# Scores and sums folded into the runs of values from block 4 on, with the output's halves in another order, in a fused attention and bilinear feed-forward kernel

## The chip, the cores and the metric

One core of one Trainium2 chip. The metric is the time of one execution on the device in microseconds (us), lower is better. Executions of one kernel scatter over 1 to 2 us within a session. The span of a profile is 1.8 us shorter than the time of the same execution (302.3 against 304.1 for the kernel before), because the time also holds what lies outside the first and last instruction.

## The reference

```
q, k, v: (8, 8, 576, 64) fp32; w_a, w_b: (512, 1536); w_out: (1536, 512)
attention within chunks of 64 positions:
    attn = softmax(q k^T / 8);  o = attn v          # 64x64 per chunk and head
x = o as 4608 tokens x 512
y = ((x w_a) * (x w_b)) w_out                       # 4608 x 512, fp32
```

## The kernel before

The 4608 tokens go in 9 blocks of 512, the attention in 18 units of 256. TensorE (PE) does two kinds of work: matmuls on the full 128x128 array for the feed-forward, in a form with seven products in place of eight, and runs of small matmuls on four 64x64 tiles at once for the attention (values, scores and sums of a unit). Scores are q k^T, and their Exp on ScalarE (ACT) gives E. Sums are E times ones; two Ln and then the inverse (an Exp) on ACT make 1/sum of them. Values are E v, which VectorE (DVE) multiplies by that into x (xT). From block 2 on, a block is six groups, and a group issues its products in this order. `now` is the group itself; `last` is the group before, whose bank C is finished here.

```python
# cut: the loop over blocks K and groups i
now.p1()                       # bank A (pa); ACT then copies it to B (pb)
if last:
    last.add7()                # DVE: c_sb = pc + v_sb; then pc = pc + u_sb
chunk(chunks.get(K, chunks[4])[2 * i])          # c0 halves of the output of block K-1
if last:
    last.p3()                  # on pb; DVE multiplies pb by b_sb
attend(K, i, 0)                # attention work hung here; sums of x on DVE
now.p6()                       # on pb; ACT then copies it to u_sb
if last:
    last.p4()                  # on pc: needs add7's second instruction
    finish(last)
now.p2()                       # on pa; ACT then copies it to b_sb
chunk(chunks.get(K, chunks[4])[2 * i + 1])      # c1 halves
attend(K, i, 1)                # runs of values, scores, sums
now.p5()                       # on pb; ACT then copies it to v_sb
exps()                         # ACT: the second Exp of the scores
now.p7()                       # starts a new pc
last = now
```

The output of a block is seven products, n = 0 to 6, in two halves each: 14 halves, dealt out to the places c0 and c1 by the table `chunks`. After product 4 DVE does two instructions on its bank C (po):

```python
if n == (3 if one else 4):   # one: a form for the last block only
    nc.vector.scalar_tensor_tensor(out=rows(self.o1, hi), in0=halves(self.C),
        scalar=OUT_SCALE, in1=halves(self.v), op0=MULT, op1=ADD)      # o_sb<-po,vo_sb
    nc.vector.tensor_tensor(out=self.C, in0=self.C, in1=self.u, op=ADD)  # po<-po,uo_sb
```

`bring(U)` casts q, k and v of unit U to bf16 on POOL (GpSimd) and starts the loads of the next; `combine_x` makes four sums of x on DVE, each `s<-xT` or `s<-s,xT` (these "sums of x" are not the attention's sums). The kernel uses eight banks of PSUM, the memory that matmuls write: pa, two pb, pc, po, pq and two pt.

The softmax here doesn't subtract the row's maximum and nothing guards it: scores larger than these inputs give would overflow.

## Time and profile before

| | before |
|---|---|
| time, median of 3 | 303.82 us (303.5 to 304.27) |
| span of the profile | 302.3 us |
| PE, DVE, ACT, POOL busy | 97, 69, 65, 64% |
| runs on 64x64 tiles from block 4 on | 9.30 us, in 16 runs |
| PE waiting between full-tile matmuls, 90 to 284 us | next to nothing |

The prediction below reads the page. I show here only lines that it doesn't show: PE in group 4 of the kernel before (start in us, duration, engine, line, operation, output<-inputs, tile, number of matmuls):

```profile
191.97 1.47 PE L578 MATMUL pq<-wo,so 128*128 128x256 f16 x12
193.28 0.60 PE L440 MATMUL pb<-s,wa 128*128 128x256 f16 x4
193.72 0.60 PE L440 MATMUL pb<-s,t 128*128 128x256 f16 x4
194.16 0.60 PE L440 MATMUL pc<-xT,t 128*128 128x256 f16 x4
```

The way to read these: the lines are two output halves, p3, p6 and p4. Durations overlap (p3 is 0.60 long, and p6 starts 0.44 after it), so the difference of two starts is the cost; where it is longer than the matmuls between need, I call the excess a step. 193.72 - 193.28 = 0.44 is one product of four matmuls, and 193.28 - 191.97 = 1.31 two output halves. No line carries a bracket with a wait.

### The profile page before, as it was taken

To read this page: it belongs to the slowest core of one execution; us is meant where nothing else is said; L and a number is where in the kernel's file an instruction comes from. 1 tells how busy PE (TensorE), PEld (TensorE's weight loads), DVE (VectorE), ACT (ScalarE), POOL (GpSimd) and SP (SyncE) were. 2 spreads that over 40 slices of the span, in tenths; PEclk is the share of its full clock that TensorE was granted. 3 is DMA by queue.
4 is the path that set the end of the run, shared out by engine and by line. 5 is a ranking of instruction groups with operands and counts; after the bars stand their busy time and mean duration, and the time that the engine had idled before them with its cause. 6 is when DMAs were issued, how large, how long until landed. Compare 5 with 4: busy or idle time off the path is not lost.

```text
span 302.3 us, 8608 instructions
## 1 busy us (share of the span) xinstructions
PE 292.4 (97%) x3527; PEld 231.9 (77%) x3527; DVE 210.0 (69%) x343; ACT 196.5 (65%) x355; POOL 193.3 (64%) x180
## 2 busy tenths in 40 slices
PE   6799999999999999999999999999999999999995
PEld 2344367866588888888888888888888888888884
DVE  3456575878767696769676966796679667965773
ACT  2643567348387768776867687768776876566532
POOL 0665758995999698808880888178817901780660
PEclk9999999999999999999999999999999999999999
DMA  7999999999999999896959395958721001100024
GB/s 222 307 382 284 283 336 345 242 217 210 219 239 262 213 242 276 188 210 181 208 122 245 129 205 132 210 163 198 123 87 72 2 2 69 73 0 3 2 98 179
DMA packets 141127, 54.29 MB, mean 180 GB/s; under 512 B 117152, under 2 KB 135200, under 8 KB 141088
## 3 DMA queue, kind: packets, MB, share of 16 engines
q1 hardware_dynamic: 140944, 53.69, 69.9%
q8 instruction: 27, 0.44, 0.6%
q14 instruction: 12, 0.10, 0.1%
q10 hardware_dynamic: 144, 0.07, 0.1%
HBM read 37.75 MB, written 9.44 MB: 156 GB/s over the span
## 4 chain that ended last, share of the span: by engine, by line
PE 83%; DMA 5%; SPq 4%; DVE 3%; POOL 1%; ACT 1%; issue 1%; DVEq 0%; ACTq 0%; POOLq 0%
PE pb L440 19%; PE pc L440 12%; PE pa L440 12%; PE po L578 12%; PE pq L578 10%; PE pb L651 3%; DMA st<-in_k_dram 3%; DMA st<-in_moe_w_b_dram 2%; PE po L390 2%; PE pc L390 2%; PE pa L390 2%; PE pq L390 2%; PE pt L328 2%; PE pt L295 2%; SPq L112 1%; SPq L194 1%
## 5 line engine op out<-in xcount | busy, mean ns | idle before, releaser
L520 POOL TENSOR_TENSOR so<-ab_sb 128x512 f16<-128x512 f16 x23 | 27.4, 1190 | 68.5 <-DVE ab_sb L490 68.5
L440 PEld LDWEIGHTS <-t 128*128 128x128 f16 x504 | 48.3, 98 | 8.4 <-issue 1.7
L440 PE MATMUL pb<-s,wa 128*128 128x256 f16 x336 | 50.5, 273 | 0.0
L440 PE MATMUL pa<-xT,wb 128*128 128x256 f16 x336 | 50.4, 273 | 0.0
L478 DVE TENSOR_TENSOR c_sb<-pc,v_sb 128x512 f32<-128x512 f32 x42 | 28.9, 687 | 27.7 <-ACT v_sb L451 27.7
L578 PEld LDWEIGHTS <-ab_sb 128*128 128x128 f16 x390 | 37.8, 98 | 5.2 <-issue 0.9
L440 PEld LDWEIGHTS <-wb 128*128 128x128 f16 x336 | 32.9, 98 | 4.0
L440 PEld LDWEIGHTS <-wa 128*128 128x128 f16 x336 | 31.8, 98 | 4.3 <-issue 0.2
L490 DVE SCALAR_TENSOR_TENSOR ab_sb<-pc,c_sb 128x512 f16<-128x512 f32 x42 | 29.0, 690 | 7.8 <-PE pc L440 6.3
L451 ACT COPY u_sb<-pb 128x512 f32<-128x512 f32 x42 | 24.7, 588 | 14.9 <-PE pb L440 14.7
L490 DVE SCALAR_TENSOR_TENSOR ab_sb<-pb,b_sb 128x512 f16<-128x512 f32 x42 | 28.9, 689 | 6.1 <-PE pb L440 5.2
L458 ACT COPY pb<-pa 128x512 f32<-128x512 f32 x42 | 24.1, 573 | 10.3 <-PE pa L440 10.0
L578 PEld LDWEIGHTS <-so 128*128 128x128 f16 x288 | 28.1, 98 | 3.4
L451 ACT COPY b_sb<-pa 128x512 f32<-128x512 f32 x42 | 25.0, 595 | 7.1 <-PE pa L440 7.1
L479 DVE TENSOR_TENSOR pc<-pc,u_sb 128x512 f32<-128x512 f32 x42 | 28.9, 688 | 0.0
L520 POOL TENSOR_TENSOR so<-so,ab_sb 128x512 f16<-128x512 f16 x23 | 27.4, 1192 | 1.7
L451 ACT COPY v_sb<-pb 128x512 f32<-128x512 f32 x42 | 24.7, 587 | 5.1 <-PE pb L440 4.4
L520 POOL TENSOR_TENSOR ab_sb<-ab_sb 128x512 f16<-128x512 f16 x23 | 26.8, 1166 | 0.0
L520 POOL TENSOR_TENSOR so<-ab_sb,so 128x512 f16<-128x512 f16 x23 | 26.1, 1163 | 0.0
L338 DVE TENSOR_TENSOR xT<-pt,ln 128x512 f16<-128x512 f32 x29 | 18.8, 685 | 9.9 <-PE pt L328 6.5
L440 PE MATMUL pb<-s,t 128*128 128x256 f16 x168 | 25.3, 273 | 0.0
L440 PE MATMUL pc<-xT,t 128*128 128x256 f16 x168 | 25.2, 272 | 0.1
(129 smaller groups left out, 574.4 us busy)
## 6 DMA issues: line engine op xcount, KB each, us to landing
out_dram<-o_sb SPq DMA_DIRECT2D x34, 256.0 KB, 2.3
st<-in_v_dram SPq DMA_DIRECT2D x32, 256.0 KB, 4.7
st<-in_k_dram SPq DMA_DIRECT2D x25, 256.0 KB, 4.5
st<-in_q_dram SPq DMA_DIRECT2D x23, 256.0 KB, 3.7
st<-in_moe_w_b_dram SPq DMA_DIRECT2D x6, 512.0 KB, 7.1
st<-in_moe_w_a_dram SPq DMA_DIRECT2D x6, 512.0 KB, 7.0
st<-in_moe_w_out_dram SPq DMA_DIRECT2D x6, 512.0 KB, 6.4
st<-in_q_dram SPq DMA_DIRECT2D x4, 512.0 KB, 5.7
```

The source lines that it names most:

```text
L295: nc.tensor.matmul(sm[cl][j * 64:j * 64 + 64, :], ones[cl * 64:cl * 64 + 64, :], E[cl * 64:cl * 64 + 64, j].rearrange("p m g s -> p (m g s)"),
L338: nc.vector.tensor_tensor(out=x.rearrange("p m (g c s) -> p m g c s", g=2, c=2)[:, m, :, cl, :], in0=av[cl][:, m], in1=rs[:, cl, m].rearra ...
L390: nc.tensor.matmul(ps[n], w_ab[n, i][:, kt, o:o + 128], xT[:, kt, c0:c1], start=(kt == 0), stop=(kt == NKT - 1),)
L440: nc.tensor.matmul(t[:, h * 256:h * 256 + 256], w[:, kt, h * 128:h * 128 + 128], x[:, kt], start=start and h == 0 and kt == 0, stop=h == 1 ...
L451: nc.scalar.copy(out=t, in_=src)
L458: nc.scalar.copy(out=self.B, in_=self.A)
L478: nc.vector.tensor_tensor(out=self.c, in0=self.C, in1=self.v, op=ADD)
L479: nc.vector.tensor_tensor(out=self.C, in0=self.C, in1=self.u, op=ADD)
L490: nc.vector.scalar_tensor_tensor(out=self.dst[:, :, c0:c0 + 256], in0=t.rearrange("p (h n) -> p h n", h=2), scalar=AB_SCALE, in1=o.rearran ...
L520: (eng or nc.gpsimd).tensor_tensor(out=o, in0=x0, in1=x1, op=op)
L578: nc.tensor.matmul(t[:, c0:c0 + 256][:, cols], a[:, kt, th * 128:th * 128 + 128], w[:, kt, cols], start=n in (0, 4) and first and kt == 0, ...
L651: nc.tensor.matmul(out_ps[K, tg], ab_tiles[K][:, ft, tg * 128:tg * 128 + 128], wo_sb[:, ft], start=(ft == 0), stop=(ft == NFT - 1),)
```

## The change

The intent is to have fewer runs on 64x64 tiles, as each pays a way in and a way out on PE (0.093 and about 0.11 us, worked out in the prediction). From block 4 on, the scores of the unit two on and the sums of the next unit go into the same run as the values. For that the scores move to bank pc and the sums to pa and one of po or pq, and the output's halves are placed so that those banks are free. The core of the diff:

```diff
+    late_ln = []
+
-    def sums(U, halves=None):
+    def sums(U, halves=None, pools=(None, None)):
         E = E_of[U]
-        sm = [bank() for _ in range(2)]
+        sm = [bank(p) for p in pools]
 # cut: with pools given, the second Ln goes to late_ln and is issued after the next p1
-                at(K, 0, 0, sums, U)
-            at(K, 1, 0, inverse, U)
+                if K == 3:
+                    at(K, 0, 0, sums, U)
+            if K == 4:
+                at(K, 0, 1, sums, U)
+                at(K, 0, 1, scores_beside(psum_c), U + 1)
+            at(K, 1, 1 if K == 4 else 0, inverse, U)
             at(K, 2, 1, values, U)
 # cut: K < 4 as before; from 4 on:
+                at(K, 2, 1, scores_beside(psum_c), U + 2)
+                at(K, 2, 1, sums_beside(psum_o), U + 1)
             at(K, 4, 1, values, U + 1)
+                at(K, 4, 1, scores_beside(psum_c), U + 3)
+                at(K, 4, 1, sums_beside(psum_q), U + 2)
 # the table of halves; a pair is (c1, c2), c2 being a new place between p5 and p7
-            4: (1, 1, 1, 1, 2, 1, 1, 2, 2, 0, 1, 1),
-            NBLK - 1: (1,) * 12,
+            3: (1, 1, 1, 1, 2, 1, 1, 2, 2, 0, 1, 1),
+            4: (0, 1, 1, (1, 1), 1, (1, 1), 1, 1, 1, (1, 1), 0, 1),
+            5: (1, 1, 1, (1, 1), 1, (1, 1), 1, 1, 1, (1, 1), 0, 1),
+            NBLK - 1: (1, 1, 1, (1, 1)) + (1,) * 8,
 # casts and loads on POOL and SP; cut: bring() takes the names to cast
-                    bring(2 * K + 4)
-                elif i == 3 and K > 2:
-                    bring(2 * K + 5)
+                    bring(2 * K + 4 if K < 4 else 2 * K + 5, "qkv" if K < 4 else "qk")
+                elif i == 3 and K == 3:
+                    bring(11)
                 elif i == 3:
 # cut: the lines that this one replaces
+                    bring(9, "qk") if K == 2 else cast(2 * K + 5, "v")
+                elif i == 5 and K > 2:
+                    bring(2 * K + 6)
 # product 5 of the output before product 4
-                        lambda g=g, n=n, th=th: g.part(n, th) for n in range(7) for th in range(2)
+                        lambda g=g, n=n, th=th: g.part(n, th)
+                        for n in (range(7) if K < 4 else (0, 1, 2, 3, 5, 4, 6))
+                        for th in range(2)
 # cut: the lines that read c0, c1 and c2 from the table; after p1, p2 and p5
-                chunk(chunks.get(K, chunks[4])[2 * i])
+                chunk(c0)
-                chunk(chunks.get(K, chunks[4])[2 * i + 1])
+                chunk(c1)
+                chunk(c2)
```

More of the change, by code (lines that the diff above doesn't have):

```diff
@@ L303, in sums @@
         rs_of[U] = ln_of[U]
+        ln = ln_of[U]
         for cl in range(2):
-            nc.scalar.activation(
-                out=ln_of[U][:, cl].rearrange("p m n -> p (m n)"), in_=sm[cl], func=AF.Ln
-            )
+            late_ln.append(
+                lambda cl=cl: nc.scalar.activation(
+                    out=ln[:, cl].rearrange("p m n -> p (m n)"), in_=sm[cl], func=AF.Ln
+                )
+            )
+        for cl in range(1 if pools[0] else 2):
+            late_ln.pop(0)()
             if halves:
@@ L355, in slot, with bring @@
             values(f)
-    def bring(U):
+    def bring(U, names="qkv"):
         if U >= NU:
@@ L363, in bring @@
         transpose_dma(U)
-        bring_v(U)
+        if "v" in names:
+            bring_v(U)
     def bring_v(U):
@@ L841, in scores_beside, with sums_beside @@
             return lambda u: scores(u, (pool, psum_b[0]), 1)
+        def sums_beside(pool):
+            return lambda u: sums(u, pools=(psum_a, pool))
         for K in range(2, NBLK):
@@ L851 @@
                 attention[K, 0, 1] = [lambda K=K: combine_x(K, (3,))]
-                at(K, 0, 0, sums, U)
-            at(K, 1, 0, inverse, U)
-            at(K, 2, 1, values, U)
-            at(K, 2, 1, scores_beside(psum_o), U + 1)
-            at(K, 3, 0, sums, U + 1)
+                if K == 3:
[4 more added lines that the diff above has]
+            at(K, 1, 1 if K == 4 else 0, inverse, U)
+            at(K, 2, 1, values, U)
+            if K < 4:
+                at(K, 2, 1, scores_beside(psum_o), U + 1)
+                at(K, 3, 0, sums, U + 1)
+            else:
+                at(K, 2, 1, scores_beside(psum_c), U + 2)
+                at(K, 2, 1, sums_beside(psum_o), U + 1)
             at(K, 3, 1, inverse, U + 1)
             at(K, 4, 1, values, U + 1)
-            at(K, 4, 1, scores_beside(psum_q), U + 2)
+            if K < 4:
+                at(K, 4, 1, scores_beside(psum_q), U + 2)
+            else:
+                at(K, 4, 1, scores_beside(psum_c), U + 3)
+                at(K, 4, 1, sums_beside(psum_q), U + 2)
             at(K, 5, 0, lambda u: combine_x(u // 2, (0,)), U + 1)
@@ L886 @@
                 if i == 1:
-                    bring(2 * K + 4)
-                elif i == 3 and K > 2:
-                    bring(2 * K + 5)
+                    bring(2 * K + 4 if K < 4 else 2 * K + 5, "qkv" if K < 4 else "qk")
+                elif i == 3 and K == 3:
+                    bring(11)
                 elif i == 3:
-                    cast(9, "qk")
-                    load(10)
-                    transpose_dma(9)
+                    bring(9, "qk") if K == 2 else cast(2 * K + 5, "v")
+                elif i == 5 and K > 2:
+                    bring(2 * K + 6)
                 if i == 0:
@@ L896 @@
                     outs += [
-                        lambda g=g, n=n, th=th: g.part(n, th) for n in range(7) for th in range(2)
-                    ]
+                        lambda g=g, n=n, th=th: g.part(n, th)
+                        for n in (range(7) if K < 4 else (0, 1, 2, 3, 5, 4, 6))
+                        for th in range(2)
+                    ]
+                steps = chunks.get(K, chunks[5])[2 * i:2 * i + 2]
+                c0, c1, c2 = steps[0], *(steps[1] if type(steps[1]) is tuple else (steps[1], 0))
                 now = Group(K, i)
                 now.p1()
+                while late_ln:
+                    late_ln.pop(0)()
                 if last:
                     last.add7()
-                chunk(chunks.get(K, chunks[4])[2 * i])
+                chunk(c0)
                 if K == 2 and i == 0:
```

## The prediction

> **What bounds the kernel now.** I read the page first: the busy line, the slices, the chain that ended last.
>
> ```profile
> PE 292.4 (97%) x3527; PEld 231.9 (77%) x3527; DVE 210.0 (69%) x343; ACT 196.5 (65%) x355; POOL 193.3 (64%) x180
> ...
> PE   6799999999999999999999999999999999999995
> ...
> PE 83%; DMA 5%; SPq 4%; DVE 3%; POOL 1%; ACT 1%; issue 1%; DVEq 0%; ACTq 0%; POOLq 0%
> ```
>
> PE is full from the second slice on and is 83% of the chain. The other engines stand at 64 to 69%, so they matter only where one of them makes PE wait. As matmul ends are modelled, "full" says little; I therefore read the timeline of PE by its start times (start, us, engine, line):
>
> ```profile
> 186.51 0.82 PE L578 MATMUL pq<-wo,so 128*128 128x256 f16 x6
> 187.16 0.60 PE L440 MATMUL pb<-s,wa 128*128 128x256 f16 x4
> 187.69 0.41 PE L295 MATMUL pt<-E,ones 64*64 64x512 bf16 x4
> 188.03 0.61 PE L440 MATMUL pb<-s,t 128*128 128x256 f16 x4
> ...
> 194.59 0.60 PE L440 MATMUL pa<-xT,wb 128*128 128x256 f16 x4
> 195.12 0.44 PE L328 MATMUL pt<-E,v_raw 64*64 64x64 bf16 x32
> 195.79 0.61 PE L440 MATMUL pb<-s,wa 128*128 128x256 f16 x4
> ```
>
> A half of an output product (x6) takes 187.16 - 186.51 = 0.65, a feed-forward product (x4) 0.437; both are 0.1093 a matmul. From 90 to 284 us I found no longer step between full-tile matmuls than that, beyond 0.04. The rest is the runs on 64x64 tiles. Sums alone: 188.03 - 187.16 - 0.437 = 0.436, of which entry is 0.093 and the rest two matmul pairs and the way out. Values with scores: 195.79 - 194.59 - 0.437 = 0.763. A block of six groups (from 184.52 to 214.47, both values) is 29.95, of which 27.6 is full-tile work, and the two kinds of runs 2 x (0.436 + 0.763) = 2.40.
>
> **What the Trainium skill says.** "TensorEngine Tiling (Array Packing)", Key Properties: "Changing tiling mode (not just tile) drains the TensorE". The trace agrees: each run pays 0.093 to get in, and after the last sums matmul 0.333 passes where its 512 columns alone take 0.22, so about 0.11 to get out. "TensorE: Matmul & The Clock Gate", Part 3, What overlaps and what doesn't: matmuls are strict FIFO; Architectural detail: ACT and DVE are strict FIFO too. So a matmul that waits holds up every later one, and a DVE instruction put ahead of another delays it. The trace shows both below. For what a matmul on these small tiles costs, I use the trace (32 in 0.253).
>
> **The change, part by part.** No instruction is added, dropped or resized on any engine. What moves is their order (I laid the two instruction lists side by side, engine by engine).
>
> 1. *Fewer runs.* From block 4 on there were 8 runs of sums, 7 of values with scores, 1 of values alone: 8 x 0.436 + 7 x 0.763 + 0.471 = 9.30. Now: sums 10 with scores 11; six runs of values, scores and sums; values 16 with sums 17; values 17. The turn from values to scores inside a run costs 0.763 - 0.471 - 0.253 = 0.04; I give the turn to sums 0.05. Appending sums then costs 0.05 + 0.010 + (0.333 - 0.119) = 0.274, where 0.119 is the old tail after scores: six runs x 1.037, two x about 0.74, and 0.471: 8.18. Gain **1.12 us**, 0.16 for each of seven runs saved. PE is the bound, so it counts in full.
>
> 2. *The fourth product of the output on DVE.* Its second half (po, the bank C) now runs between p5 and p7 of group 4, and group 5 has no half after its first product. When that bank is done, DVE has to do four things in order. The same four stand in the trace before, after two halves in group 3:
>
> ```profile
> 190.92 0.69 DVE L626 SCALAR_TENSOR_TENSOR o_sb<-po,vo_sb 128x512 f32<-128x512 f32 x1 [1.11 <-PE po L578]
> 191.65 0.70 DVE L630 TENSOR_TENSOR po<-po,uo_sb 128x512 f32<-128x512 f32 x1
> 192.25 0.68 DVE L478 TENSOR_TENSOR c_sb<-pc,v_sb 128x512 f32<-128x512 f32 x1
> 192.85 0.69 DVE L479 TENSOR_TENSOR pc<-pc,u_sb 128x512 f32<-128x512 f32 x1
> ```
>
> From the first start to the last end 2.62; it began 0.26 after the last matmul of po had given way (190.66 to 190.92). The product p4 accumulates into pc and so needs the last of the four. That it does wait can be seen where PE stalled early on:
>
> ```profile
> 86.46 0.69 DVE L479 TENSOR_TENSOR pc<-pc,u_sb 128x512 f32<-128x512 f32 x1
> ```
>
> ```profile
> 86.47 0.60 PE L440 MATMUL pb<-s,t 128*128 128x256 f16 x4
> 87.20 0.60 PE L440 MATMUL pc<-xT,t 128*128 128x256 f16 x4
> ```
>
> DVE ends at 87.15, PE goes on at 87.20: 0.05. In the old order PE had two more halves (1.31) in between, and p4 came at 194.16, after 193.54. In the new order only p7, p1, p3 and p6 lie between: 4 x 0.437 = 1.75. The chain is 0.26 + 2.62 + 0.05 = 2.93. PE idles 2.93 - 1.75 = 1.18 in group 5, in blocks 4, 5, 6 and 7: **4.7 us**. The missing half also leaves p6 waiting for ACT's copy of pa into pb (the copy starts 0.31 after the start of p1's last matmul, takes 0.57; p6 could have started 0.38 earlier), but that lies inside the same 1.18.
>
> 3. *The first group of block 4.* It has no half after p1 either, so p6 waits 0.38 for that copy. And its run is sums 10, then scores 11 into pc. ACT does two Ln first, then the Exp that frees pc for p7. In the trace ACT's Ln pair starts 0.43 after the sums (202.67 to 203.11) and each next instruction 0.49 later, so Exp ends at 0.43 + 0.98 + 0.60 = 2.01 from the sums' start; p7 is due at 0.27 + 0.25 + 0.12 + 0.437 = 1.08. Wait with the 0.05: 0.97. With 0.08 for p4 in the next group: **1.4 us**, once.
>
> 4. *The scores in pc elsewhere.* There Exp is the first on ACT and a half stands before p7. From the run's end Exp ends at 0.49, p7 is due at 1.09. Hidden. The Ln of pa ends at 0.99, p1 is due at 1.53. The second Exp and copy end near 2.77, p6 of group 3 is due at 3.06. Hidden, by 0.3.
>
> 5. *End.* In the last block C is now ready in group 5, so the pair of DVE instructions stands before the last pair of c_sb and pc: STT at 0.26, then as above, end 2.88 after p5's start, p4 due at 2.62: 0.31, against 0.04 before: **0.3 us**.
>
> 6. *Elsewhere.* In group 0 the last output eviction (0.69, 0.60 to the next) now stands between add7 and p3's multiply. I walk it: add7 at 0.43 and 1.04 after p1, eviction 1.64, multiply 2.24, one sum of x (0.41 to 0.65), multiply of pc to 3.9 to 4.2; p7 is due at 3.93. Up to 0.3 in five blocks; I take **0.4 us** in all. Casts moved on POOL: needed products lie 4 us or more after; loads and transposes keep some 14 us. Hidden.
>
> Sum: 303.8 - 1.1 + 4.7 + 1.4 + 0.3 + 0.4 = 309.5. As part 6 and a share of 3 may vanish in slack I did not see, I state 309.2, 1.8% slower.
>
> **The rivals.** *The intent wins*: the waits are hidden and only 1.1 is saved, 302.7. For it: the order of halves was plainly chosen to give banks time, and the same table shows care for p7. Against it: the four DVE instructions cannot be shortened, and nothing but four products covers them. *ACT becomes the bound around the merged runs*: the Ln moved ahead of v_sb and the copy. At 65% busy it has room, and the walk of part 4 leaves 0.3; if I mis-sized that by 0.3, 7 groups lose as much, 2 us more, 311. *Transfers*: scores a unit earlier need q and k earlier. The DMA is at 1.00 of its time around 110 us and 0.84 by 135, where the first of them is loaded; a late landing would hold up POOL, then the output, once, by a few us. POOL's idle stretch of 7.8 us a block speaks against it.
>
> **Range and chances.** The four stalls of part 2 are the surest term (each within 0.15, so 0.6); part 3 may be 0.8 to 1.8; part 6 zero to 1.5; the saving 0.8 to 1.5. Together 307.2 to 310.6 for 8 times in 10. The line of 2% lies at 309.9, just above my number: slower by over 2% three times in ten. Faster by 2% would need 6 us that a saving of at most 1.5 cannot give; I leave 0.02 for an error of mine in the whole reading.
>
> **What would show it.** In the profile after: runs of values, scores and sums of about 1.04; on PE in group 5 of blocks 4 to 7 a step of 1.2 us before p4 (pc<-xT,t), with the DVE instruction on pc,u_sb as its releaser; a wait of some 1 us for Exp on pc once, near 144 us; blocks of 29.95 - 0.32 + 1.2 = 30.8. No such step at p4 would prove part 2 wrong, and with it the number: blocks of 29.6 and 303. Steps at p6 or p1 released by ACT would favour the second rival, POOL or a DMA as releaser of the output's halves the third.

## The result, and the profile after

The changed kernel took 310.91 us (median of 4, 310.08 to 311.97) against 303.66 (303.34 to 304.27) for the kernel before in the same rounds: a ratio of 1.0238 (1.0202 to 1.0274). Ratios here are the recorded ones of the runs in the same rounds, with their 95% interval, so not quite the ratio of the medians I quote. Executions over 1.5% slower than the fastest of the same kernel are left out of the means. Two later sessions gave 1.0215 (1.0193 to 1.0237) and 1.0196 (1.0165 to 1.0226). So the change costs 6.0 to 7.2 us, and the first session's median lies 0.3 us above the range that I had given. Over the kernel before, that range was 3.4 to 6.8 us: 7.2 lies above it, the later 6.5 and 6.0 inside, so on which side the result fell was in part scatter.

PE's busy slices and the chain that ended last, on the page after:

```profile
PE   6699999999999999998999899989998999899995
...
PE 77%; DVE 7%; DMA 7%; SPq 4%; issue 1%; ACT 1%; POOL 1%; DVEq 0%; POOLq 0%
```

From the third slice to the last but one all were 9; now five are 8, each 7.7 us long: the one from 139 us on, at the turn from block 3 to 4, and those from 170, 201, 232 and 263 us on, one in each of blocks 4 to 7. And DVE's share of the chain has gone from 3 to 7%. The view of PE's waits says on what (who waited for whom: us in all, how often, the longest):

```profile
PE pc L448 <- DVE pc L487: 2.7, 5, 0.6
PE pb L448 <- ACT pb L466: 1.3, 5, 0.3
...
PE pc L448 <- ACT E L279: 0.8, 1, 0.8
```

In the kernel before, none of these stands among the twelve largest. The wait alone comes out less than the lost time (0.53 against 0.69 at p4 below), so I count by start times. Group 5 of block 5 on PE after (the output's half with product 4 ends here, as it ended before group 4 in the kernel before):

```profile
199.49 0.82 PE L586 MATMUL po<-wot,ab_sb 128*128 128x256 f16 x6
200.14 0.60 PE L448 MATMUL pc<-s,t 128*128 128x256 f16 x4
200.58 0.60 PE L448 MATMUL pa<-xT,wb 128*128 128x256 f16 x4
201.02 0.60 PE L448 MATMUL pb<-s,wa 128*128 128x256 f16 x4
201.89 0.60 PE L448 MATMUL pb<-s,t 128*128 128x256 f16 x4 [0.28 <-ACT pb L466]
203.02 0.60 PE L448 MATMUL pc<-xT,t 128*128 128x256 f16 x4 [0.53 <-DVE pc L487]
...
204.54 0.60 PE L448 MATMUL pb<-s,wa 128*128 128x256 f16 x4
205.29 0.60 PE L448 MATMUL pc<-s,t 128*128 128x256 f16 x4
```

p6 starts 0.87 after p3 instead of 0.44, p4 1.13 after p6: 0.43 and 0.69 lost, 1.13 together. The last two lines are p5 and p7: p7 starts 0.75 after p5, a step of 0.31. DVE in the same stretch of the same kernel:

```profile
200.34 0.69 DVE L634 SCALAR_TENSOR_TENSOR o_sb<-po,vo_sb 128x512 f32<-128x512 f32 x1 [0.44 <-PE po L586]
201.07 0.70 DVE L638 TENSOR_TENSOR po<-po,uo_sb 128x512 f32<-128x512 f32 x1
201.68 0.68 DVE L486 TENSOR_TENSOR c_sb<-pc,v_sb 128x512 f32<-128x512 f32 x1
202.27 0.69 DVE L487 TENSOR_TENSOR pc<-pc,u_sb 128x512 f32<-128x512 f32 x1
...
203.47 1.17 DVE L428 TENSOR_TENSOR s<-xT 128x512 f16<-128x512 f16 x1
204.56 0.68 DVE L498 SCALAR_TENSOR_TENSOR ab_sb<-pc,c_sb 128x512 f16<-128x512 f32 x1
```

This is the chain of four instructions that the prediction laid out, from 200.34 to 202.96, and PE goes on 0.06 later. What was not in it is the line before the last: a sum of x that takes 0.41 when alone took 1.17. The last line is the multiply that frees pc; it ended at 205.24, and p7 went on 0.05 later. POOL's instruction beside the sum, same kernel:

```profile
203.32 1.04 POOL L213 CAST v_raw<-st 128x1024 bf16<-128x1024 f32 x1
```

Blocks 6 and 7 have no casts in group 5, as the last of the 18 units has been cast before. There the same sum was short in both profiles of the changed kernel (0.41 to 0.42), and p7 had no step. Group 5 of block 6, profile after:

```profile
234.79 0.42 DVE L428 TENSOR_TENSOR s<-xT 128x512 f16<-128x512 f16 x1
```

From the run in group 2 of one block to that of the next it is 31.28 and 31.32 over the group 5 of blocks 4 and 5, and 30.82 over that of block 6; the prediction had 30.8 for all.

The merged run before that, on PE after (the scores' lines left out):

```profile
197.38 0.82 PE L586 MATMUL po<-wot,ab_sb 128*128 128x256 f16 x6
198.13 0.44 PE L335 MATMUL pt<-E,v_raw 64*64 64x64 bf16 x32
...
199.04 0.61 PE L448 MATMUL pb<-s,wa 128*128 128x256 f16 x4
```

It costs 199.04 - 197.38 - 0.655 (the half ahead of it) = 1.005, where values with scores (0.763) and sums alone (0.436) made 1.199 before: 0.19 saved here. The six merged runs took 1.00 to 1.05, so 0.15 to 0.19 each.

The whole account, from start times on PE (start minus start before minus the matmuls between). The second column of results is a second profile of the same changed kernel, whose time was 310.44:

| term | predicted | profile after | second profile |
|---|---|---|---|
| fewer runs (9.30 before; 8.05 and 8.00 after) | -1.12 | -1.25 | -1.30 |
| group 5 of blocks 4 to 7, p6 and p4 | +4.7 | +4.53 | +4.53 |
| turn from block 3 to 4: p7, p6, p4, p7 | +1.4 | +2.27 | +1.45 |
| end | +0.3 | 0.0 | 0.0 |
| p7 in group 5 of blocks 4 and 5, and in the group 0 after each | +0.4 | +1.04 | +1.05 |
| p4 in group 4 of blocks 4 to 7 | 0 | +0.43 | +0.42 |
| sum | 5.7 | 7.0 | 6.2 |
| measured from block 2's first values to the end, less 208.5 before | | 7.0 | 6.3 |

The last row leaves out the loading phase, which ends between 93.0 and 96.1 us in the profiles and so adds up to some 3 us that no kernel explains. At the end p4 waits 0.25 instead of 0.04 as predicted, but a later wait for po is 0.15 instead of 0.37, so nothing is left of it.

### The profile page after: what moved, and what is told of

The parts are those of the page before. It is cut to its first block, busy times and chain, and to the rows that moved or that the text cites. A ratio compares the mean times of both kernels' runs of the same rounds, so it can differ in the third digit from the quotient of the medians.

```text
span 309.0 us, 8602 instructions
## 1 busy us (share of the span) xinstructions
PE 293.6 (95%) x3525; PEld 232.0 (75%) x3527; DVE 212.2 (69%) x343; ACT 196.4 (64%) x355; POOL 193.5 (63%) x180
## 4 chain that ended last, share of the span: by engine, by line
PE 77%; DVE 7%; DMA 7%; SPq 4%; issue 1%; ACT 1%; POOL 1%; DVEq 0%; POOLq 0%
PE pb L448 16%; PE pc L448 12%; PE po L586 11%; PE pa L448 11%; PE pq L586 10%; DMA st<-in_q_dram 3%; PE pb L659 3%; DMA st<-in_v_dram 2%; PE po L398 2%; SPq L182 2%; DMA st<-in_moe_w_b_dram 2%; PE pa L398 2%; DVE c_sb L486 2%; PE pq L398 2%; DVE s L428 2%; DVE pc L487 2%
## 5 line engine op out<-in xcount | busy, mean ns | idle before, releaser
L528 POOL TENSOR_TENSOR so<-so,ab_sb 128x512 f16<-128x512 f16 x23 | 26.6, 1159 | 1.7
L448 PE MATMUL pc<-s,t 128*128 128x256 f16 x168 | 25.2, 272 | 1.3 <-ACT E L279 0.8
```

What stands on the lines that cost most here:

```text
L448: nc.tensor.matmul(t[:, h * 256:h * 256 + 256], w[:, kt, h * 128:h * 128 + 128], x[:, kt], start=start and h == 0 and kt == 0, stop=h == 1 ...
L528: (eng or nc.gpsimd).tensor_tensor(out=o, in0=x0, in1=x1, op=op)
```

## The experiments

Fourteen runs on three chips. My theory after the first look: the DVE chain in front of p4 costs 4.5 of the loss, the rest comes from POOL's casts that stretch DVE's sums of x, and from the turn into block 4. Rivals: the merged runs themselves (their banks and their work on ACT), and the loading of q and k a unit earlier.

**e1_casts: the casts moved away from group 5.**

```diff
                 if i == 1:
+                    if K >= 4:
+                        cast(2 * K + 4, "v")
                     bring(2 * K + 4 if K < 4 else 2 * K + 5, "qkv" if K < 4 else "qk")
-                elif i == 5 and K > 2:
-                    bring(2 * K + 6)
+                elif i == 4 and K > 2:
+                    bring(2 * K + 6, "qk")
```

> The changed kernel with the casts of q and k for the unit after next at the start of group 4, where POOL was idle, instead of group 5, and the cast of v two groups later. Nothing on PE, ACT or DVE moves. Theory (POOL's casts in group 5 stretch DVE's sums of x from 0.41 to about 1.2 us, so the multiply that frees pc comes late): the sums of x in groups 5 and 0 go back to 0.4 to 0.7, the steps of 0.3 before p7 in group 5 and most of 0.64 before p4 at the start of block 4 go; 1.2 to 1.9 us less than the changed kernel, near 309.3. Rival (DVE simply has too many instructions there): under 0.4 less, 310.5 or more. The step of 1.13 before p4 in group 5 stays under both.

Measured 311.32 us (311.01 to 312.82), before 304.27 (303.62 to 304.95): 1.0247 (1.0214 to 1.0281). In its trace the steps at p7 in group 5 of blocks 4 and 5 and after are gone, but the 0.64 before p4 at the turn stayed and the time did not fall: the expectation failed. As it had run beside the kernel before and not beside the changed one, I ran the same file twice more, below.

**e2_no_add: the second of the four DVE instructions taken out** (wrong: relative error 0.66).

```diff
-                nc.vector.tensor_tensor(out=self.C, in0=self.C, in1=self.u, op=ADD)
+                if one or not 3 <= self.K < 7:
+                    nc.vector.tensor_tensor(out=self.C, in0=self.C, in1=self.u, op=ADD)
```

> The changed kernel without the addition po<-po,uo_sb on DVE in blocks 4 to 7 (wrong result on purpose, 4 instructions of 0.60 from start to start fewer). Theory (the chain of four DVE instructions sets p4 in group 5): p4 in group 5 comes 0.60 earlier, so the steps before p6 and p4 together shrink from 1.13 to about 0.53, and the step before p7 may shrink by up to 0.3: 2.4 to 3.5 us less, near 308. Rival (ACT's copy of pa into pb, which makes p6 wait 0.44, or the long runs themselves hold PE): 1 us less or none, as only 0.69 of each 1.13 would be DVE's at most and the rest of the sum would reappear elsewhere.

Measured 308.74 us (308.22 to 308.92), 1.0143 (1.0124 to 1.0163), so 2.2 to 2.9 us less than the changed kernel at its 1.0215 to 1.0238 (2.4 to 3.5 were expected). PE in group 5, profile of e2_no_add:

```profile
201.97 0.60 PE L448 MATMUL pb<-s,t 128*128 128x256 f16 x4 [0.28 <-ACT pb L466]
202.41 0.60 PE L448 MATMUL pc<-xT,t 128*128 128x256 f16 x4
```

p4 follows p6 by 0.44, with no wait: the 0.69 is gone in all four blocks, 4 x 0.69 = 2.8. The wait of p6 for ACT stays at 0.44, as it should, since it has another cause. At p7 some shifted: the step in group 0 grew from 0.2 to 0.46, that in group 5 fell from 0.31 to 0.02. That the chain on DVE sets p4 is thereby shown, not only read.

**e3_split: the sums back in runs of their own**, everything else as changed.

```diff
-                if K == 3:
+                if K != 4:
                     at(K, 0, 0, sums, U)
-                at(K, 2, 1, sums_beside(psum_o), U + 1)
+                at(K, 3, 0, sums, U + 1)
-                at(K, 4, 1, sums_beside(psum_q), U + 2)
```

> The changed kernel with its order of halves, but sums 11 to 17 back in runs of their own in groups 3 and 0 (into the two pt banks); scores stay two units on. Theory (a saved run is worth what the trace says, 0.763 + 0.436 - 1.007 = 0.19): seven more runs cost 1.3, of which some 0.3 may come back since sums in group 0 give DVE time: 0.7 to 1.4 us more than the changed kernel, near 312. Rival (the merged runs bring new waits on ACT that eat their saving): no change or less, 311 or below.

Measured 311.12 us (309.92 to 312.21), 1.0224 (1.019 to 1.0257): level with the changed kernel, where 0.7 to 1.4 us more were expected. The runs cost 9.28 again, yet the steps at p7 were absent, and p4's at the turn into block 4 was 0.11 in this profile. The casts lay in group 5 as before, but in block 5 the sum of x began 0.10 ahead of the cast of v (202.00 against 202.10) and took 0.43. So the merging by itself is not what makes the kernel slower; its gain of 1.25 and the waits at p7 of about 1.0 nearly cancel. That is read from start times.

**e4_halves: the kernel before with only the table and the order of the halves changed.**

```diff
-            4: (1, 1, 1, 1, 2, 1, 1, 2, 2, 0, 1, 1),
-            NBLK - 1: (1,) * 12,
+            3: (1, 1, 1, 1, 2, 1, 1, 2, 2, 0, 1, 1),
+            4: (0, 1, 1, (1, 1), 1, (1, 1), 1, 1, 1, (1, 1), 0, 1),
+            5: (1, 1, 1, (1, 1), 1, (1, 1), 1, 1, 1, (1, 1), 0, 1),
+            NBLK - 1: (1, 1, 1, (1, 1)) + (1,) * 8,
 # and the order 0, 1, 2, 3, 5, 4, 6, and chunk(c2), as in the change
```

> The kernel before with only the new places and the new order of the output halves from block 4 on; scores one unit on, sums in their own runs, casts where they were. Theory (the order of halves is what costs: 1.13 in group 5 of four blocks, 0.4 at the start of block 4, 0.25 at the end, 0.1 to 0.3 elsewhere): 5 to 6.5 us more than the kernel before, near 309.3. Rival (halves alone are harmless, and the runs with their ACT and POOL order bring the loss): within 1.5 us of the kernel before.

Measured 309.57 us (309.33 to 310.12), 1.0176 (1.0156 to 1.0197): 5.35 us more than before. The steps on PE are the same 0.44 at p6 and 0.69 at p4 in each of four blocks, and 0.18 at p4 in group 4. At the turn into block 4 there is 0.05 only. The order of the halves alone makes three quarters of the loss or more.

**after_again: the changed kernel once more**, five rounds, as the basis for what follows on this chip.

> The changed kernel as it is, on the chip of the next three, since the profiled executions start their steady part up to 1.4 us apart and e1 needs a reference of the same chip. Expected 7.0 to 7.5 us over the kernel before if the first measurement was sound.

Measured 310.74 us (310.0 to 311.11), before 304.36 (303.15 to 304.95): 1.0215 (1.0193 to 1.0237), 6.5 us over it where 7.0 to 7.5 were expected. What its profile shows beside the first is told below.

**e5_old_halves: the changed kernel with the old order and nearly the old table.**

```diff
-            4: (0, 1, 1, (1, 1), 1, (1, 1), 1, 1, 1, (1, 1), 0, 1),
-            5: (1, 1, 1, (1, 1), 1, (1, 1), 1, 1, 1, (1, 1), 0, 1),
-            NBLK - 1: (1, 1, 1, (1, 1)) + (1,) * 8,
+            5: (1, 1, 1, 1, 1, (1, 1), 1, 2, 2, 0, 1, 1),
+            NBLK - 1: (1,) * 12,
-                        for n in (range(7) if K < 4 else (0, 1, 2, 3, 5, 4, 6))
+                        for n in range(7)
```

> The changed kernel with the order and the places of the output halves of the kernel before (one of three halves of group 2 stays between p5 and p7); merged runs, scores two units on and casts as in the changed kernel. Theory (the halves cost 5.4, of which the merged runs are innocent): no step before p4 in group 5; what stays is 1.3 of wait for Exp and some tenths at the start of block 4, up to 0.2 per merged run in group 4, where no half stands before p7, against 1.2 saved: 0 to 2 us over the kernel before, near 305. Rival (merged runs need the new order of halves, whose places were chosen for them): waits of 0.5 us and more at p7, p1 or p6 after each run, 4 us or more over the kernel before.

Measured 306.87 us (305.99 to 307.25), 1.0087 (1.0069 to 1.0106): 3.9 less than the changed kernel, but 2.6 over the kernel before where 0 to 2 were expected. No step before p4 in group 5. At the turn into block 4 the steps were 0.38, 0.36, 1.09, 0.30 and 0.40 (p7, p4, p7, p3, p4). And the merged run in group 4 now took 1.18 instead of 1.005, as the sums wait 0.17 for ACT's copy that frees pa; with that the merging in that group saves only 0.02 of 1.199. As I read it, this is what the new order of the halves bought: time for pa at one place, paid for on DVE at another.

**e6_old_casts: e5 with the casts of e1 and the scores of unit 11 put ahead of the sums of unit 10 in block 4.**

```diff
-                at(K, 0, 1, sums, U)
                 at(K, 0, 1, scores_beside(psum_c), U + 1)
+                at(K, 0, 1, lambda u: sums(u, pools=(psum_t, psum_t)), U)
 # and the edits of e1_casts and e5_old_halves
```

> As e5_old_halves, with the casts at the start of group 4 and, in the first group of block 4, scores 11 ahead of sums 10 and the second Ln after the next copy. Theory (saved runs are worth 1.2 once their waits are gone): the wait of 1 us for Exp falls to 0.1, steps before p7 go; 0.5 to 1.2 us less than the kernel before, near 303. Rival (a merged run moves its cost to ACT whatever the order): same as the kernel before or slower.

Measured 304.91 us (304.21 to 306.13 for the fast runs), 1.0026 (1.0002 to 1.005): not the 0.5 to 1.2 us less than the kernel before that was expected, but 0.8 more. One of its runs, the profiled one, took 310.57 and counts as slow. ACT and PE there, profile of e6_old_casts:

```profile
154.97 0.60 ACT L609 ACTIVATE o_sb<-po 128x512 f32<-128x512 f32 x1 [4.20 <-DMA out_dram<-o_sb]
```

```profile
157.03 0.95 PE L448 MATMUL pb<-s,wa 128*128 128x256 f16 x4 [4.27 <-ACT v_sb L459]
157.79 1.06 PE L448 MATMUL pb<-s,t 128*128 128x256 f16 x4
158.64 1.06 PE L448 MATMUL pc<-xT,t 128*128 128x256 f16 x4
```

A store of the output had been queued on SP behind a load and two transposes of the casts that I had moved; ACT needed its buffer, PE needed ACT. Then PE did four matmuls in 0.85 instead of 0.44, for about 3.4 us. The Trainium skill, "TensorE: Matmul & The Clock Gate", Part 1, What's actually happening, has PE's clock halved after one idle window of about 3.4 us and restored after a busy one of the same length; the trace agrees, with 4.3 us idle before it and a granted clock of 0.50 from 158 to 160 us. This is my edit's fault, not that of the change; whether the fast executions of e6 lost anything there is not shown.

**e7_casts_k4: the changed kernel with the casts of e1 and the turn of e6, the new halves kept.**

```diff
-                at(K, 0, 1, sums, U)
                 at(K, 0, 1, scores_beside(psum_c), U + 1)
+                at(K, 0, 1, lambda u: sums(u, pools=(psum_t, psum_t)), U)
 # and the edit of e1_casts
```

> The changed kernel with its own halves, casts at the start of group 4 and the first group of block 4 turned round as in e6. Theory: what is left over the kernel before is the halves' 5.4 less the 1.2 that runs save, plus 0.4 to 1 at the start of block 4: 4.5 to 5.2 us over the kernel before, 2 to 2.7 less than the changed kernel. Rival (time is lost in the start phase or elsewhere, as e1's time did not fall): 6.5 us or more over the kernel before.

Measured 308.31 us (307.79 to 309.95), 1.0148 (1.0123 to 1.0172): 2.4 less than the changed kernel, and 4.5 over the kernel before, as expected. The wait for Exp at the turn fell from 1.0 to 0.1.

**f1_store_first: e6 with the casts, loads and transposes of group 4 issued after its first half**, so that the store goes ahead.

```diff
-                elif i == 4 and K > 2:
-                    bring(2 * K + 6, "qk")
                 chunk(c0)
+                if i == 4 and K > 2:
+                    bring(2 * K + 6, "qk")
```

> As e6_old_casts, but the casts of group 4 (and the loads and transposes that stand with them in the queue) come after the half that ends an output eviction, so its two stores stand ahead of them in the DMA queue. In e6's profile ACT waited 4.2 us for a store that stood behind loads and transposes, and PE with it. Theory (a queue served in order, not the merged runs, made that wait): no step over 1 us after 90 us; 303.6 to 304.4, level with the kernel before, since merged runs in group 4 wait 0.17 for ACT's copy of pa and so save 0.02 instead of 0.19. Rival (the wait comes from late loads, wherever the store stands): a step of over 2 us stays, time as e6 or more.

Measured 303.97 us (303.72 to 305.1), before 304.37: 1.0004 (0.9984 to 1.0024). With the halves, the casts and the turn all put right, the kernel is level with the one before. The merging now saves 0.19 in three runs of group 2 and nothing in those of group 4 (1.18), while the turn into block 4 still has steps of 1.1 together.

**f2_one_merged: f1 with merged runs in group 2 only.**

```diff
-                if K == 3:
+                if K != 4:
                     at(K, 0, 0, sums, U)
-                at(K, 4, 1, scores_beside(psum_c), U + 3)
-                at(K, 4, 1, sums_beside(psum_q), U + 2)
+                at(K, 4, 1, scores_beside(psum_q), U + 3)
```

> As f1_store_first, but sums join only the run of group 2; in group 4 the run is values and scores (into pq and pb) as in the kernel before, and sums stand alone in group 0 again. Theory: four runs saved at 0.19, less some 0.4 at the start of block 4: 0.2 to 0.6 us less than the kernel before at best, 303.4 to 304.2, not to be told from it. Rival (any change of this kind costs): 305 or more.

Measured 304.01 us (303.15 to 305.3), 1.0005 (0.9981 to 1.0029). Level too; I found no version that beats the kernel before beyond the scatter.

**f3_k4: the changed kernel with only the turn of e6.**

```diff
-                at(K, 0, 1, sums, U)
                 at(K, 0, 1, scores_beside(psum_c), U + 1)
+                at(K, 0, 1, lambda u: sums(u, pools=(psum_t, psum_t)), U)
```

> The changed kernel with one part undone: in the first group of block 4, scores 11 come ahead of sums 10 (so Exp, which frees pc, is first on ACT) and the second Ln follows the next copy. Theory (Exp behind two Ln makes p7 wait 1.0 once): 0.8 to 1.0 us less than the changed kernel, 309.6 to 310.2 here if the kernel before stands at 304.2. Rival: under 0.3 less.

Measured 310.23 us (308.7 to 311.53), 1.0204 (1.0176 to 1.0233). In the trace the Exp now stands ahead of the Ln, and p7's step is 0.1 instead of 1.0; the time shows 0.3 to 0.5 less than after_again, inside the scatter, where 0.8 to 1.0 were expected. From block 2's first values to the end its profile took 213.6 against 214.8 of after_again. The wait is proved, its worth in the time of executions is not resolved.

**f4_casts, g1_after and g2_casts: e1 again, beside the changed kernel.** No new edit: f4 and g2 are e1's file, g1 is the changed kernel's. f4 ran on the chip of after_again in a later session, beside f3; g1 and g2 in the same rounds on a third chip.

> e1_casts once more, in more rounds: its profile lost the steps before p7 (1.1 us less from the run at 93 to the last run), yet its time did not fall. Theory: 0.7 to 1.3 us less than the changed kernel, 309.5 to 310.1 if the kernel before stands at 304.2. Rival (the casts only move the loss to late loads at the start of block 4): 310.5 or more, and large steps near 140 to 155 us.

> The changed kernel once more, beside g2 on the same chip and in the same rounds. 6.4 to 7.3 us over the kernel before.

> e1_casts (the same file as f4_casts) beside the changed kernel on the same chip. Theory (POOL's casts stretch DVE's sums of x in group 5 and this delays the multiply that frees pc): 0.8 to 2 us less than g1, and the sums of x in group 5 of blocks 4 and 5 at 0.7 or less. Rival (what the casts gain is lost again near the start of block 4, as e1's time said): within 0.5 us of g1.

f4: 308.95 us (307.77 to 309.64), 1.0156 (1.0128 to 1.0183), where after_again had 1.0215. g1: fast runs 309.03 to 311.23, 1.0196 (1.0165 to 1.0226); its profiled run took 866 us, with its matmuls at a fraction of their rate, and is not used; the others lie 6.0 over the kernel before, just under the 6.4 expected. g2: 309.06 us (308.27 to 311.09), 1.0153 (1.0126 to 1.0181). By these ratios moving the casts gains 1.8 us on one chip and 1.3 on the other, though the intervals of g1 and g2 overlap. A third pair is e7 and f3, which differ in the casts alone: 1.0148 (1.0123 to 1.0172) against 1.0204 (1.0176 to 1.0233), 1.7 us. The steps at p7 that go away had cost 1.04. The sum of x of the view above is short again, profile of g2_casts:

```profile
204.34 0.41 DVE L428 TENSOR_TENSOR s<-xT 128x512 f16<-128x512 f16 x1
```

e1's first runs showed none of this. Its profile tells a part of why: the moved casts waited 5.1 and 1.2 us for the loads of q and k, POOL's own sums so came late and ran beside DVE's sum of x at the turn (1.14), and ACT waited 0.85 for a store. The steps at the turn (p6, p4, p7, and p6 of group 2) were 0.38, 0.64, 1.01 and 0.50, 1.1 more than in after_again or f4. In g2 and e7 they come to 2.2 and 2.5 likewise, in f4 to 1.4, so the rival (what the casts gain is lost again near the start of block 4) is right for some executions. How often, the record does not show.

## Why the prediction was right, and where it was not

The direction and the main term held, the size came out too low: 309.2 with a top of 310.6, measured 310.91 in the first session (310.74 and, for the fast runs, 310.09 later). The 0.3 us that I took off my sum of 309.5 for slack went the wrong way.

**Part 1, fewer runs: right.** 1.25 to 1.30 saved against 1.12; a merged run costs 1.00 to 1.05 against 1.037.

**Part 2, the four DVE instructions: right.** 1.13 in each of four blocks against 1.18, as DVE began 0.20 after p7's start instead of 0.26, with the releasers named beforehand, among them the wait of p6 for ACT inside the same sum. e2 took the second instruction out and p4 moved up by 0.69; e4 had the same steps with no merged run at all.

**Part 3, the turn into block 4: right in one profile, 0.8 short in the other.** The Exp's 0.97 came as 0.95 and 1.00, p6's 0.38 as 0.384. But p4 of this first group, for which I had nothing, came 0.644 late in the first profile and 0.061 in the second; the "0.08 for p4 in the next group" came in neither. The two profiles are of the same program, and the difference is which of two instructions came first. DVE and POOL in the first profile:

```profile
141.26 1.04 DVE L428 TENSOR_TENSOR s<-s,xT 128x512 f16<-128x512 f16 x1
```

```profile
140.99 1.04 POOL L213 CAST v_raw<-st 128x1024 bf16<-128x1024 f32 x1
```

And in the second (after_again):

```profile
141.43 0.56 DVE L428 TENSOR_TENSOR s<-s,xT 128x512 f16<-128x512 f16 x1
```

```profile
141.66 1.23 POOL L213 CAST v_raw<-st 128x1024 bf16<-128x1024 f32 x1
```

In the first the cast began 0.27 ahead and DVE's sum stretched to 1.04, while the cast took its usual 1.04. In the second the sum began 0.23 ahead and took 0.56 (the cast before it, of k, ran on until 141.71), while the cast stretched to 1.23. The sum stands in front of add7 on DVE and so in front of p4. The Trainium skill, "SBUF — State Buffer", Who interferes with whom, states the rule for this: a DVE instruction with two inputs in SBUF contends with a GpSimd instruction that reads SBUF, over shared ports that are an exclusive lock, and the order of issue decides who blocks. The sums have both inputs in SBUF and the casts read SBUF, so the page applies; add7, with one input in PSUM, kept its 0.68 to 0.69 beside the casts of group 5, which agrees too. The first profile has a step of 0.30 at the p7 just before as well, the second has none: there the cast of q began 0.09 ahead of the sum of x (1.24), in the second both began at 139.41 and the sum took 0.42.

**Part 6 is the step that failed.** It said "Casts moved on POOL: needed products lie 4 us or more after" and "Hidden": I asked only whether the casts come in time for those who use them, not what they do to DVE while they run. I took "one sum of x (0.41 to 0.65)", from the stretch around 200 us. The trace before had the warning in it: at 79 to 82 us, beside POOL's casts and sums, three sums of x took 1.25 to 1.37. The change puts three casts of a unit in group 5, just where DVE, late from its four instructions, does its sums and then the multiply that frees pc for p7. A sum stretched to 1.17, the multiply came late, and p7 waited 0.31 in group 5 of blocks 4 and 5; in the group 0 after each a sum took 0.82 behind one of POOL's own sums, which the casts had pushed later, and p7 waited 0.2. Together 1.04 against the 0.4 that I gave to all of "Elsewhere". The turn's 0.30 and 0.64 of the first profile have the same cause, so an execution can lose up to about 0.9 us more or less by who starts first. That the casts do this is shown: the steps at p7 are absent from block 6's group 5 on, where no casts lie, and in e1, f4 and g2, where they lie elsewhere. What moving them is worth in time is less sure (1.3 to 1.8 in three pairs, nothing in e1).

**Not in the prediction at all: p4 in group 4**, 0.11 in each of four blocks, 0.43. In the trace v_sb stands on ACT behind the inverse (1.06), as in the kernel before, but the new table puts one half less there, so add7 starts late. e4, which has the table and no merged run, shows the step too (0.18), so it belongs to the halves; e5, with the old table, has no step there. That it is the missing half I read, and did not test by itself.

**Part 5, the end:** the predicted wait came (0.25 against 0.04), and a later one fell by as much; net nothing.

**The rivals.** "The intent wins" fell with part 2. "ACT becomes the bound around the merged runs" did not come: with the new halves the runs were about as long as predicted. It came only in e5, where the old order made the sums wait 0.17 for ACT's copy of pa, which is why the halves could not simply be put back. "Transfers" gave no wait in the two profiles of the changed kernel worth naming, but with the casts moved they did: ACT waited 0.85 for a store in e1, and in e6 a store behind loads cost that one execution 4.3 us of PE time and the slow matmuls after it.

In sum: the order of the halves costs 5.35 (e4, measured alone), the merging gives back 1.25 to 1.30 (read from start times), the turn into block 4 costs some 1.4 (read; not resolved in time by f3), and the casts 1.0 (read) to 1.8 (measured). That makes 6.5 to 7.3, against 6.0 to 7.2 measured over three sessions; the terms overlap by what e4 already holds of the turn and the end.

## What to carry to other kernels

A saving on the bounding engine is worth only what the reordering that makes it possible leaves over: here 1.25 us of mode changes were bought with an order that left PE 1.75 us of work to hide 2.9 us of DVE's. Before moving instructions, count for every bank how much PE work lies between the last write of one and the first use after it, and compare it with all that is queued on the engine that must touch the bank in between. And when work moves on one engine, ask not only whether its result is in time, but which instructions of other engines it will run beside.

## What the Trainium skill lacked or had wrong

- "SBUF — State Buffer", Who interferes with whom: agrees, and explained what I had missed; it lacks the size for a pair like this. Here a sum of x that takes 0.41 alone took 1.04 and 1.17 behind a cast of 1.04, ending 0.27 to 0.28 after the cast, or else the cast took 1.23 behind a sum of 0.56. Which one it was at the turn changed from one execution of the same program to the next.
- "TensorEngine Tiling (Array Packing)", Key Properties: names the drain at a change of tiling mode but no cost. Here it is 0.093 us in and about 0.11 out, and a run saved by merging was worth 0.15 to 0.19.
- "TensorE: Matmul & The Clock Gate", Part 1, Wait — 56ns, not 53.3ns?: "Start-to-start never drops below ≈25 ns" needs the words "on one tile". On four 64x64 tiles 32 matmuls take 0.253 us, about 8 ns from start to start. Part 3 of the page has a figure for packed tiles, but none for this mode with these sizes.
- No page that I read gives the time from one engine's end to another's start. Here PE went on 0.05 to 0.06 after DVE's end, and DVE's first instruction on po began 0.20 to 0.26 after PE's next product had started, ACT's copy of pa 0.31 to 0.36 after the start of p1's last matmul.
